# Loading twelve dense partial sums from another engine's queue, with a new table of ranks

## The chip, the core and the metric

The kernel runs on one core of one Trainium2 chip. The metric is the device time of one launch in microseconds (us). Three runs of the kernel before took 374.27, 373.19 and 374.27 us, so its time is 374.27 us (the median).

A core has five engines with instruction streams of their own: TensorE (PE, matrix products), VectorE (DVE), ScalarE (ACT), GpSimd (POOL) and SyncE (SP). Each takes its instructions strictly in the order in which they are written. Transfers (DMAs) are issued by an engine, here by SP and POOL, and then run beside it; a transfer that adds into its target is issued by POOL in this kernel.

## What is computed

The reference mixes, by a gate per row, a spectral filter and a two-layer perceptron. Shapes: A_x and B_x are 1 x 2048 x 512, w1 is 512 x 1792, w2 is 1792 x 512.

```python
x = A_x
g = _sigmoid((x * gate_w).sum(-1, keepdims=True))
X = jnp.fft.rfft2(x, axes=(-2, -1)) * (A_w_r + 1j * A_w_i)
a = jnp.fft.irfft2(X, s=(S, D), axes=(-2, -1))
h = jax.nn.gelu(jnp.einsum("bsd,df->bsf", B_x, w1) + b1, approximate=True)
b = jnp.einsum("bsf,fd->bsd", h, w2) + b2
return g * a + (1 - g) * b
```

Both reference branches see the same x here. Every product is made of three with split operands (a high and a low part: high x high, high x low, low x high).

## The kernel before

**How the work is cut.** The 2048 rows are four chunks of 512, `c` = 0 to 3. The 1792 hidden columns are 14 blocks of 128 (`f`), taken in two halves of seven. `mlp(half, c)` makes, for one chunk and one half, the up-projections `ph` (12 matmuls of 128 x 512 for each `f`), the gelu on ACT, the split into `g..h` (ACT) and `g..l` (DVE), and the down-projections `po` for four blocks `q` of 128 output columns (3 matmuls for each `f`). The first half's negated result goes to a buffer in device memory, `bacc[c]`. The second half's result is added to it there by POOL (`bacc<-o`), since no buffer on the chip holds it so long. The second halves run in the order of chunks 3, 0, 1, 2. The input of a chunk, split into `mxh` and `mxl`, exists once: the next chunk's, 1 MB each (`mxh<-xs2h`, `mxl<-xs2l` for chunk 2), may only be loaded once the last `ph` of the chunk before is done.

**The spectral part.** `forward` (16 blocks of rows) does the real transform along columns (`pd`) and rows (`py`) on PE; `stage1` and `filt` combine and filter on DVE; `stage4(c)` starts the inverse on DVE (names beginning with `d` and a digit, then `y`). `inverse(c, h)` makes for a half chunk two groups `pz` from `v..h` and `v..l` (PE; ACT makes `sw` and `v..h`, DVE `pq` and `v..l`), splits them into `z..h` and `z..l`, makes `pa` from those (PE), copies half of it to `od` (ACT), and takes sum and difference `uv` (DVE). The result goes to `out` by plain transfers on SP and by additions on POOL (`out<-uv`, `out<-y`).

**The step that is changed.** `combine(c, h)` (line 1037), called for chunks 3, 0 and 1, brings the finished dense sums back: for each of the two `k` it loads 256 KB of `bacc[c]` into a buffer `ba`, of which there are two slots. DVE scales it in place by the gate less one (line 1045). Then for chunks 3 and 0 POOL adds it to `out` (`out<-ba`), for chunk 1 with `h` = 0 SP writes it to `out` and the spectral part is added later, and for chunk 1 with `h` = 1 DVE adds it to `y` on the chip (line 1024). That is 3 x 2 x 2 = 12 loads. A load must wait for the two additions into `bacc` that it reads, and for its slot, which becomes free when the addition or write to `out` of the content before has landed.

**Chunk 2 is done last, and its end differs.** Its first-half result is loaded as `bb`. For `q` below 2 DVE makes `oo` from it (two buffers, lines 1142 and 1144) and POOL adds them to `out` (`out<-oo`). For `q` of 2 and 3 DVE makes the output tiles `o` (lines 1167 and 1172) from `po` and the finished `y`. `o` and `oo` share the two slots of one pool, `so`: the tile `o` of `q` = 2 may only be written once the transfer of the first `oo` has landed. The last matmuls of all are two groups of `po` for `q` = 3, each 256 wide (`po_230` and `po_23256`).

**What sets the order.** The program is first a list of 1,870 steps, each with its engine, its buffers and a rank. A planner (`Graph.schedule`) runs through estimated time and always starts, on each engine, the step of lowest rank among those whose inputs and slots are ready; the order that comes out is the order in which the instructions are written. The ranks come from a table, `RANKS`, one number for each step:

```python
for s, r in zip(g.steps, RANKS):
    s.rank = r / 100
order = g.schedule()
```

A step on SP takes part in the plan through `dma`, with at most 8 transfers in flight (`hw`); a step on POOL through `dma_pool` (plain) and `acc` (adding), with at most 3 in flight (`ring`).

Of the kernel before, what the change touches and what calls it, by code (L numbers as in the profile page):

```python
# [17 lines left out]
P = 128  # L18
# [154 lines left out]
class Graph:  # L173
# [282 lines left out]
def tile_kernel(ctx: ExitStack, tc: tile.TileContext, xt, w1, w2, b1, b2, x0g, wf, wrev, out, consts):  # L456
# [58 lines left out]
    def dma_pool(dst, src, kb, reads, writes, rank=FEED):  # L515
        reads = [*reads, buf("ring", [1], cls=len(g.steps))]
        return add("pool", kb / 300, 3.2, lambda: nc.gpsimd.dma_start(dst(), src()), reads, writes, rank)  # L517
# [772 lines left out]
```

## Time and profile before

The profile is of one more execution. A trace has a row for each instruction: its start, its duration, its line, what it writes and reads, and in brackets the time that its engine sat idle before it, with what ended that time.

| | |
|---|---|
| time, median of 3 runs (lowest, highest) | 374.27 us (373.19, 374.27) |
| the profiled execution's own time | 375.86 us |
| its span, first to last instruction | 374.1 us |
| mean granted TensorE clock | 0.998 |
| POOL busy, instructions | 53.2 us, 66 |
| loads `ba<-bacc` on POOL, each 256 KB | 12, first at 222.39 us, last at 347.94 us |
| DMA packets, bytes | 48564, 62.99 MB |

Three times stand beside one another: 375.86 us for the profiled execution, 374.1 us for its span, and 374.27 us for the median of the runs without a profile. A difference that is worked out from the trace is a difference in the first two.

### The profile page before, as it was taken

To read this page: it belongs to the slowest core of one execution; us is meant where nothing else is said; L and a number is where in the kernel's file an instruction comes from. 1 tells how busy PE (TensorE), PEld (TensorE's weight loads), DVE (VectorE), ACT (ScalarE), POOL (GpSimd) and SP (SyncE) were. 2 spreads that over 40 slices of the span, in tenths; PEclk is the share of its full clock that TensorE was granted. 3 is DMA by queue.
4 is the path that set the end of the run, shared out by engine and by line. 5 is a ranking of instruction groups with operands and counts; after the bars stand their busy time and mean duration, and the time that the engine had idled before them with its cause. 6 is when DMAs were issued, how large, how long until landed. Compare 5 with 4: busy or idle time off the path is not lost.

```text
span 374.1 us, 5563 instructions
## 1 busy us (share of the span) xinstructions
PE 365.5 (98%) x1838; PEld 310.0 (83%) x1838; DVE 326.6 (87%) x691; ACT 227.8 (61%) x454; POOL 53.2 (14%) x66
## 2 busy tenths in 40 slices
PE   7999999999999999999999999999999999999993
PEld 6888888888888888888888888888888877888893
DVE  4999999999999788999999999597758595999986
ACT  5766587876679735473467122984786449549820
POOL 0000000000000002011032021003323233312150
PEclk9999999999999999999999999999999999999999
DMA  8962799524965218479298952338958896854295
GB/s 284 377 183 89 213 289 337 169 84 141 268 191 152 64 16 218 120 162 229 66 232 206 308 79 43 57 109 239 208 96 145 191 286 163 129 102 123 86 128 153
DMA packets 48564, 62.99 MB, mean 168 GB/s; under 512 B 4656, under 2 KB 28272, under 8 KB 47760
## 3 DMA queue, kind: packets, MB, share of 16 engines
q1 hardware_dynamic: 40232, 46.39, 38.5%
q0 software_dynamic: 8160, 15.99, 26.0%
q8 instruction: 14, 0.23, 0.2%
q10 hardware_dynamic: 144, 0.26, 0.2%
q14 instruction: 14, 0.11, 0.1%
HBM read 38.64 MB, written 23.73 MB: 167 GB/s over the span
## 4 chain that ended last, share of the span: by engine, by line
PE 77%; DVE 8%; ACT 6%; DMA 6%; issue 2%; SPq 0%; DVEq 0%; POOL 0%; POOLq 0%; ACTq 0%
PE ph L530 35%; PE po L530 32%; PE pd L530 4%; PE py L530 3%; PE pz L530 2%; ACT sw L949 2%; PE pa L530 2%; DMA ba<-bacc 1%; DMA out<-oo 1%; DVE uv L1002 1%; DMA xr<-in_xt 1%; DMA out<-uv 1%; ACT sw L952 1%; DVE y L812 1%; DVE y L1021 1%
## 5 line engine op out<-in xcount | busy, mean ns | idle before, releaser
L1105 ACT ACTIVATE ph<-ph,b1t 128x512 f32<-128x512 f32 x56 | 36.7, 656 | 47.4 <-PE ph L530 47.3
L949 ACT ACTIVATE sw<-y,al 64x512 f32<-64x512 f32 x32 | 22.9, 722 | 3.3 <-DVE y L812 2.5
L521 POOL DMA_DIRECT2D wa7l<-in_w x1 | 1.0, 1007 | 141.3 <-PE po L530 141.3
L956 DVE SCALAR_TENSOR_TENSOR pq<-y,al,sw 128x256 f32<-128x256 f32 x32 | 14.6, 480 | 7.2 <-ACT sw L952 7.1
L908 DVE TENSOR_TENSOR m<-y,wf 128x514 f32<-128x514 f32 x32 | 20.6, 689 | 0.2
L521 POOL DMA_DIRECT2D bacc<-o x12 | 11.1, 926 | 54.2 <-ACT o L1154 54.2
L1154 ACT ACTIVATE o<-po 128x512 f32<-128x512 f32 x12 | 7.1, 594 | 15.4 <-PE po L530 15.4
L1151 ACT ACTIVATE o<-po,b2t 128x512 f32<-128x512 f32 x16 | 10.8, 684 | 9.0 <-PE po L530 8.9
L764 ACT ACTIVATE y<-pys 64x257 f32<-64x257 f32 x24 | 10.0, 418 | 5.4 <-DVE pys L761 5.0
L517 POOL DMA_DIRECT2D ba<-bacc x12 | 9.2, 764 | 26.3 <-DMA out<-ba 13.1
L530 PE MATMUL pd<-cf,eoh 128*128 128x260 f32 x64 | 12.6, 288 | 0.1
L1002 DVE TENSOR_TENSOR uv<-pa,od 128x512 f32<-128x512 f32 x16 | 10.4, 684 | 2.3 <-ACT od L999 2.3
L688 DVE TENSOR_TENSOR eo<-xr 128x256 f32<-128x256 f32 x30 | 12.0, 418 | 0.0
L530 PEld LDWEIGHTS pd<-cf,eoh 128*128 128x128 f32 x64 | 10.3, 189 | 1.2 <-issue 0.3
L999 ACT ACTIVATE od<-pa 128x512 f32<-128x512 f32 x8 | 4.8, 595 | 9.6 <-PE pa L530 9.4
L530 PE MATMUL pd<-cf,eol 128*128 128x130 f32 x64 | 10.4, 252 | 0.0
L952 ACT ACTIVATE sw<-y 1x512 f32<-1x512 f32 x16 | 10.0, 628 | 0.4
L530 PEld LDWEIGHTS pd<-cf,eol 128*128 128x128 f32 x64 | 9.8, 189 | 0.2
L702 DVE TENSOR_TENSOR xr<-eo 128x256 f32<-128x256 f32 x24 | 9.6, 418 | 0.1
L1045 DVE SCALAR_TENSOR_TENSOR ba<-gb,ba 128x512 f32<-128x512 f32 x12 | 8.2, 685 | 1.6 <-DMA ba<-bacc 1.6
L521 POOL DMA_DIRECT2D out<-ba x8 | 6.9, 863 | 15.9 <-DVE ba L1045 11.2
L650 DVE TENSOR_TENSOR mxl<-xm,mxh 128x512 fp32r<-128x512 f32 x12 | 7.8, 687 | 1.5 <-ACT mxh L649 1.5
(714 smaller groups left out, 1361.6 us busy)
## 6 DMA issues: line engine op xcount, KB each, us to landing
wf<-in_wf SPq DMA_DIRECT2D x16, 257.0 KB, 4.9
bacc<-o SPq DMA_DIRECT2D x16, 256.0 KB, 4.3
xr<-in_xt SPq DMA_DIRECT2D x15, 256.0 KB, 3.6
war<-in_w SPq DMA_DIRECT2D x14, 256.0 KB, 3.5
wbr<-in_w SPq DMA_DIRECT2D x14, 256.0 KB, 3.0
xm<-in_xt SPq DMA_DIRECT2D x12, 256.0 KB, 5.2
bacc<-o POOLq DMA_DIRECT2D x12, 256.0 KB, 4.1
ba<-bacc POOLq DMA_DIRECT2D x12, 256.0 KB, 3.4
```

The source lines that it names most:

```text
L521: return add("pool", kb / 150, 3.4, lambda: nc.gpsimd.dma_start(dst(), src(), accum_op=ALU.add), reads, writes, rank)
L530: pe.matmul(ps, w, x, start=start, stop=stop)
L688: v(lambda s=s, op=op: vec.tensor_tensor(eo.ap()[:, s], x.ap()[:, 0:2], x.ap()[:, 2:4], op=op), 256, [x], [(eo, s)], FEED)
L702: v(lambda k=k, op=op: vec.tensor_tensor(quarter(cl, k), eo.ap()[:, :, 0], eo.ap()[:, :, 1], op=op), 256, [eo], [(cl, k)] if j % 4 == 0 or ...
L764: a(lambda o=o, i=i: act.activation(Y[j].ap()[o:o + HP, 1], pys.ap()[i:i + HP, 1], AF.Copy), 257, [(pys, 1)], [(Y[j], 1 + k)], 0, more=0.1)
L908: v(lambda mk=mk, k=k, y=y, w=w: vec.tensor_tensor(mk.ap(), y.ap(), w.ap()[:, k:k + 1, :ND].to_broadcast([P, 2, ND]), op=ALU.mult), 514, [ ...
L949: a(lambda sw=sw, y=y, o=o, i=i: act.activation(sw.ap()[o:o + HP], y.ap()[i:i + HP, ::-1, :HD], AF.Copy, scale=al.ap()[i:i + HP, 0:1]), 51 ...
L952: a(lambda sw=sw, y=y, j=j: act.activation(sw.ap()[HP:HP + 1], y.ap()[HP:HP + 1, ::-1, :HD], AF.Copy, scale=math.cos(math.pi * j / NJ)), 5 ...
L956: v(lambda sw=sw, pq_=pq_, y=y, j=j, k=k, op=op: vec.scalar_tensor_tensor(pq_.ap()[:, k], y.ap()[:, k, :HD], al.ap()[:, 1 + j:2 + j], sw.a ...
L1002: v(lambda i=i, op=op: vec.tensor_tensor(uv.ap()[:, :, i], ps.ap()[:, 0], od.ap(), op=op), 512, [ps, od], [(uv, i)], 2)
L1105: a(lambda f=f, ps=ps: act.activation(ps.ap(), ps.ap(), AF.Gelu_apprx_tanh, bias=b1t.ap()[:, f:f + 1]), 600, [b1t], [ps], 0.9 if half else ...
L1151: a(lambda o=o, ps=ps, q=q: act.activation(o.ap(), ps.ap(), AF.Identity, scale=-1.0, bias=b2t.ap()[:, q:q + 1]), 600, [b2t, ps], [o])
```

## The change

`combine` issues its twelve loads of `bacc` by SP's queue and no longer by POOL's. The target, the source, the size and the declared dependences are the same. POOL is left with the adding transfers alone. All 1,870 numbers of `RANKS` are new, so the planner writes the whole program in another order; the steps themselves are the same.

```diff
 RANKS = (
-    71, 55, -369, -8, 46, 96, 146, 814, 1420, 458, 434, 906, 646, 2488, 2489, 832, 866, 912, 1011, 1123, 2161, 1407, 517,
...
+    -149, 43, 217, 3, 143, 100, 150, 574, 1118, 447, 437, 885, 624, 1856, 1001, 866, 832, 912, 1753, 1799, 1869, 396,
...
@@ combine(c, h)
         for k in range(2):
             b = buf("ba", [P, 2, 2 * P], F32, f"ba{k}{c}{h}")
-            dma_pool(lambda b=b: b.ap(), lambda k=k: bacc[c].ap()[2 * k:2 * k + 2, :, 2 * h * P:(2 * h + 2) * P].rearrange("q p n -> p q n"),
-                     256, [(bacc[c], 2 * q + h) for q in (2 * k, 2 * k + 1)], [b], 3)
+            dma(lambda b=b, k=k: sp.dma_start(
+                b.ap(), bacc[c].ap()[2 * k:2 * k + 2, :, 2 * h * P:(2 * h + 2) * P].rearrange("q p n -> p q n")),
+                256, [(bacc[c], 2 * q + h) for q in (2 * k, 2 * k + 1)], [b], 3)
```

What moves is seen in the written order at three places. In it `x2` marks a row that stands for two instructions, and the number behind a name is a buffer's.

**First place: PE, early, around the first down-projections.** The rows are the first of `po` and what follows them. Before:

```order
L530 MATMUL po_010_255<-g_0h,wb0h 128x512
L530 MATMUL po_010_255<-g_0l,wb0h 128x512
L530 MATMUL po_010_255<-g_0h,wb0l 128x512
L530 MATMUL ph_3_261<-mxh_110,wa3h 128x512
L530 MATMUL ph_3_261<-mxl_125,wa3h 128x512
```

And in the changed kernel:

```order
L530 MATMUL po_010_254<-g_0h,wb0h 128x512
L530 MATMUL po_010_254<-g_0l,wb0h 128x512
L530 MATMUL po_010_254<-g_0h,wb0l 128x512
L530 MATMUL po_010_254<-g_1h,wb1h 128x512
L530 MATMUL po_010_254<-g_1l,wb1h 128x512
L530 MATMUL po_010_254<-g_1h,wb1l 128x512
L530 MATMUL po_020_274<-g_0h,wb0h 128x512
```

The three rows that read `g_1` stood behind `ph_3` and `ph_4` and now stand right behind those of `g_0`.

**Second place: SP's queue and PE where chunk 2 takes over from chunk 1.** On SP before (`mxh` and `mxl` are chunk 2's input, `ti` small tables):

```order
L1015 DMA out<-uv_3332 128x512
L939 DMA ti_3359<-ti 128x128
L1015 DMA out<-uv_3332 128x512
L939 DMA ti_3418<-ti 128x128
L527 DMA mxh_3427<-xs2h 128x2048
L527 DMA mxl_3434<-xs2l 128x2048
```

And in the changed kernel:

```order
L1015 DMA out<-uv_3332 128x512
L1040 DMA ba_3360<-bacc_676 128x2x256
L1015 DMA out<-uv_3332 128x512
L1040 DMA ba_3388<-bacc_676 128x2x256
L939 DMA ti_3398<-ti 128x128
L527 DMA mxh_3430<-xs2h 128x2048
L527 DMA mxl_3441<-xs2l 128x2048
```

Two of the twelve loads now stand ahead of chunk 2's input in one queue. On PE a little later, before (`v2h` and `v2l` are the first operands that the inverse of chunk 2 makes):

```order
L530 MATMUL po_120_3523<-g_8h,wb8h 128x512
L530 MATMUL po_120_3523<-g_8l,wb8h 128x512
L530 MATMUL po_120_3523<-g_8h,wb8l 128x512
L530 MATMUL pz_3561<-tg_3280,v2h 128x256 x2
L530 MATMUL po_120_3523<-g_9h,wb9h 128x512
```

And in the changed kernel:

```order
L530 MATMUL po_120_3508<-g_12h,wb12h 128x512
L530 MATMUL po_120_3508<-g_12l,wb12h 128x512
L530 MATMUL po_120_3508<-g_12h,wb12l 128x512
L530 MATMUL pz_3589<-tg_3268,v2h 128x256 x2
L530 MATMUL pz_3589<-tg_3268,v2l 128x128 x2
```

Counted in the whole order, 42 matmuls of `po` stood between the last `ph` of chunk 1 and the first of chunk 2, and now 48; the first `pz` of `v2h` has moved back by 12 matmuls in all.

**Third place: POOL and DVE at the end.** POOL's last rows before:

```order
L521 DMA out<-uv_4024 128x512 x2
L521 DMA out<-oo_4054 128x512
L521 DMA out<-y 128x512
L521 DMA out<-oo_4085 128x512
L521 DMA out<-uv_4024 128x512
```

And in the changed kernel:

```order
L521 DMA out<-oo_4037 128x512
L521 DMA out<-uv_4045 128x512 x2
L521 DMA out<-oo_4063 128x512
L521 DMA out<-uv_4045 128x512
L521 DMA out<-y 128x512
```

DVE's last rows before:

```order
L1120 SCALAR_TENSOR_TENSOR bb_3947<-gb,bb_3947 128x512
L1167 SCALAR_TENSOR_TENSOR o_22_4116<-gb,po_220_4050 128x512
L1172 TENSOR_TENSOR o_22_4116<-y,o_22_4116 128x512
L1002 TENSOR_TENSOR uv_4135<-pa_4093,od_4122 128x2x256 x2
L1021 TENSOR_TENSOR y<-uv_4135 128x512 x2
L1123 TENSOR_TENSOR y<-y,bb_3947 128x2x256
L1024 TENSOR_TENSOR y<-y,ba_3971 128x512
L1024 TENSOR_TENSOR y<-y,ba_3881 128x512
L1167 SCALAR_TENSOR_TENSOR o_23_4175<-gb,po_230_4118 128x256
```

And in the changed kernel (one line was added, so line numbers are higher by one):

```order
L1121 SCALAR_TENSOR_TENSOR bb_3939<-gb,bb_3939 128x512
L1168 SCALAR_TENSOR_TENSOR o_22_4110<-gb,po_220_4033 128x512
L1173 TENSOR_TENSOR o_22_4110<-y,o_22_4110 128x512
L1124 TENSOR_TENSOR y<-y,bb_3939 128x2x256
L1002 TENSOR_TENSOR uv_4136<-pa_4100,od_4126 128x2x256 x2
L1021 TENSOR_TENSOR y<-uv_4136 128x512 x2
L1024 TENSOR_TENSOR y<-y,ba_3985 128x512
L1024 TENSOR_TENSOR y<-y,ba_3876 128x512
L1168 SCALAR_TENSOR_TENSOR o_23_4175<-gb,po_23256_4122 128x256
```

The first `out<-oo` now stands ahead of the two `out<-uv`, and the addition of `bb` to `y` ahead of the last `uv`. On PE, 39 matmuls of 256 columns follow the last `pa`, where 42 did.

216 rows, old and new, of the table RANKS are left out of this document.

## The prediction, made before the changed kernel was run

> **What bounds the kernel now.** The first view is the busy time of each engine, the second the same by stretches of the span (start and end, length, then busy time and instructions by engine, granted clock, DMA share, GB/s).
>
> ```profile
> PE 365.5 (98%) x1838; PEld 310.0 (83%) x1838; DVE 326.6 (87%) x691; ACT 227.8 (61%) x454; POOL 53.2 (14%) x66
> 9.20:130.00 120.80, 120.65 (x639) 103.77 (x640) 115.75 (x272) 87.38 (x216) 0.00 (x0) 1.00 0.65 198
> 130.00:285.00 155.00, 155.00 (x725) 129.82 (x724) 135.91 (x274) 87.32 (x149) 28.85 (x34) 1.00 0.61 148
> 285.00:320.00 35.00, 34.43 (x171) 28.46 (x170) 23.90 (x50) 22.04 (x38) 11.47 (x14) 1.00 0.88 203
> 320.00:363.50 43.50, 43.50 (x241) 37.83 (x240) 39.99 (x77) 25.70 (x45) 11.76 (x14) 1.00 0.58 112
> 363.50:374.10 10.60, 4.65 (x39) 4.44 (x38) 7.01 (x13) 0.24 (x1) 0.87 (x1) 0.93 0.63 151
> ```
>
> PE is the bound, and full: from 9.2 to 363.5 us it idles 0.15 + 0.57 = 0.7 us, at clock 1.00. The change neither adds nor removes a matmul. It can win only what PE still waits and what lies behind PE's last matmul, a couple of us; it can lose as much as it makes PE wait. POOL, whose queue is relieved, is busy 14%, so its busy time decides nothing. What matters is what the loads held up, and what they will hold up.
>
> The third view is the trace around the only idle stretch in PE's middle, on PE, SP and POOL, with the chain of waits through it (start, us, what).
>
> ```profile
> 305.94 0.39 PE L530 MATMUL ph<-mxh,wa7h 128*128 128x512 f32 x1
> 306.52 0.50 PE L530 MATMUL ph<-mxl,wa7h 128*128 128x512 f32 x1 [0.19 <-DMA mxl<-xs2l]
> 309.38 0.39 PE L530 MATMUL po<-g_8l,wb8h 128*128 128x512 f32 x1
> 309.61 0.39 PE L530 MATMUL po<-g_8h,wb8l 128*128 128x512 f32 x1
> 310.33 0.50 PE L530 MATMUL pz<-tg,v2h 128*128 128x256 f32 x2 [0.34 <-ACT v2h L576]
> ...
> 284.59 0.89 POOL L521 DMA_DIRECT2D out<-ba  x1 [0.22 <-issue]
> 292.40 0.88 POOL L521 DMA_DIRECT2D out<-y  x1 [4.65 <-ACT ph L1105]
> 293.14 0.89 POOL L517 DMA_DIRECT2D ba<-bacc  x1
> 295.53 0.42 SPq L527 DMA_DIRECT2D mxl<-xs2l  x1
> ...
> 287.05 4.68 DMA out<-uv
> 293.14 5.52 DMA ba<-bacc
> ...
> 298.76 0.69 DVE L1045 SCALAR_TENSOR_TENSOR ba<-gb,ba 128x512 f32<-128x512 f32 x1 [1.58 <-DMA ba<-bacc]
> ```
>
> A matmul of 512 columns starts 0.23 us after the one before it (309.38 to 309.61). Here two starts come late: 306.52 - 305.94 - 0.23 = 0.35 us, because chunk 2's input lands 11 us after its issue, and 310.33 - 309.61 - 0.23 = 0.49 us, because `v2h` is late. The chain says why `v2h` is: POOL's `out<-y` waited for a write of SP that landed at 291.73 (287.05 + 4.68), the load of `ba` stood behind it until 293.14 and took 5.52 us, and DVE, which scales `ba` before it starts the inverse of chunk 2, stood still for 1.58 us until it landed. So the queue that the change empties did cost PE time, in one place.
>
> The last view is the end: the chain, then DVE, ACT and PE in the trace.
>
> ```profile
> 357.96 5.48 DMA out<-oo
> ...
> 361.26 0.68 DVE L1120 SCALAR_TENSOR_TENSOR bb<-gb,bb 128x512 f32<-128x512 f32 x1
> 363.15 0.60 ACT L999 ACTIVATE od<-pa 128x512 f32<-128x512 f32 x1 [3.65 <-PE pa L530]
> 363.52 0.69 DVE L1167 SCALAR_TENSOR_TENSOR o<-gb,po 128x512 f32<-128x512 f32 x1 [1.58 <-DMA out<-oo]
> 364.25 0.69 DVE L1172 TENSOR_TENSOR o<-y,o 128x512 f32<-128x512 f32 x1
> 364.86 1.28 DVE L1002 TENSOR_TENSOR uv<-pa,od 128x512 f32<-128x512 f32 x2
> 367.38 0.69 DVE L1123 TENSOR_TENSOR y<-y,bb 128x512 f32<-128x512 f32 x1
> 367.99 1.29 DVE L1024 TENSOR_TENSOR y<-y,ba 128x512 f32<-128x512 f32 x2
> 369.19 0.74 DVE L1167 SCALAR_TENSOR_TENSOR o<-gb,po 128x256 f32<-128x256 f32 x2
> 369.85 0.76 DVE L1172 TENSOR_TENSOR o<-y,o 128x256 f32<-128x256 f32 x2
> 363.07 0.28 PE L530 MATMUL po<-g_7l,wb7h 128*128 128x256 f32 x1
> 363.19 0.28 PE L530 MATMUL po<-g_7h,wb7l 128*128 128x256 f32 x1
> 367.87 0.28 PE L530 MATMUL po<-g_13h,wb13l 128*128 128x256 f32 x1
> ```
>
> DVE stood 1.58 us until the first `out<-oo` had landed and freed the slot of `o`, and then ran without a break to 370.61. PE was done at 367.87 + 0.28 = 368.15. DVE is thus the last engine, about 1 us behind what PE alone would allow (369.19 against 368.15).
>
> **The change part by part.** *The twelve issues.* POOL loses 12 issues of 0.75 us, SP gains 12; the nearest row on SP, the load of `bb` (256 KB from the same buffer), issues in 0.33 us.
>
> ```profile
> L517 POOL DMA_DIRECT2D ba<-bacc x12 | 9.2, 764 | 26.3 <-DMA out<-ba 13.1 <-DMA bacc<-o 9.4 <-issue 3.9
> 346.17 0.33 SPq L1114 DMA_DIRECT2D bb<-bacc  x1
> ba<-bacc POOLq DMA_DIRECT2D x12, 256.0 KB, 3.4
> bb<-bacc SPq DMA_DIRECT2D x4, 256.0 KB, 3.0
> out<-ba POOLq DMA_DIRECT2D x8, 256.0 KB, 5.6
> ```
>
> They land in 3.4 us (median) from POOL, `bb` in 3.0 from SP. I take 0 for issue and landing: between 0.4 us less and nothing, twelve times, but DVE stands still for one of these loads only, in the row at 298.76 above; the others are covered by what DVE and PE do between (without that cover each would cost its 3 us). *The waits.* POOL stood 26.3 us in front of these loads. That wait does not vanish, it goes to SP, where the `uv` writes, the `ti` and the chunk inputs stand behind it; what this can cost is the second rival.
>
> The Trainium skill says, in "DMA: Bandwidth & Descriptors", section "SWDGE vs HWDGE vs iDMA", that starting transfers on several engines saves only the sequencer's time for starting them, which is usually small, since all run on the same DMA engines. By that rule the sum would be 0; by the rows the 4.65 us that POOL stood in front of `out<-y`, with a load behind it, is more than an issue.
>
> *Second place, PE's two late starts: -0.84 us.* In SP's queue the second load no longer stands behind `out<-y`. It needs the slot that the `out<-ba` of 284.59 frees; at the median of 5.6 us that is 290.2, against 293.14. DVE then need not stand 1.58 us, and the `pz` of `v2h` stands 12 x 0.23 = 2.7 us later on PE. Each alone exceeds 0.49. Chunk 2's input gets 6 more matmuls ahead of it, 1.36 us, against 0.35. Bounds: -0.53 us if only the idle time in brackets goes (0.19 + 0.34), -0.84 if the whole of both goes.
>
> *Third place, the end: -1.1 us.* On DVE the two rows of `uv` that stood ahead of the rows that make `oo` now stand behind, and so does a `v13l` that stood between: 3 rows of 0.61 us (367.38 to 367.99 is one). With `out<-oo` issued ahead of both `uv`, it starts 1.8 us sooner and lands at 357.96 + 5.48 - 1.8 = 361.6. Then DVE goes on after `bb` (361.26) at 0.61 us a row: `o` 361.87, `o` 362.48, `y` + `bb` 363.09, free at 363.70. `od` ends at 363.15 + 0.60 = 363.75, plus 3 x 0.12 us because 3 matmuls of 256 fewer follow `pa` (363.07 to 363.19 is one): 364.11. So `uv` starts at 364.15, not 364.86. From `uv` to the last `o` were 369.19 - 364.86 = 4.33 us; without the row of `bb` in it, 3.72: 367.87. The second of the last `o` must wait for PE's 368.15, so the two sums begin near 368.55, not 369.85. That is -1.3. If the `z` rows ahead of `bb` slip a little, only the 0.7 us at `uv` remain; I take -1.1, nearer the full amount, since each row but the transfer's own landing has its measured price. Next late would be PE itself.
>
> *First place and everything else: +0.4 us.* A new order of 1,870 steps makes waits that no row of before shows. Below: none, which is what 130 to 285 us had. Above: one load late by a landing, 3.2 us net (first rival). I take 0.4, near the 0.35 and 0.49 that this order's own two waits cost.
>
> Sum: -0.84 - 1.1 + 0.4 = -1.54 us. Against the profiled execution, 375.86 - 1.54 = 374.3 us (span 374.1 to 372.6). The median, 374.27, lies 1.6 us under that execution; taking the same difference, I forecast **372.7 us**.
>
> **The rivals.** *PE starves early (slower).* `g_1l` is now read right after the first `po`.
>
> ```profile
> 14.81 0.68 DVE L577 TENSOR_TENSOR g_1l<-ph,g_1h 128x512 fp32r<-128x512 f32 x1
> 15.62 0.39 PE L530 MATMUL po<-g_0h,wb0l 128*128 128x512 f32 x1
> 22.19 0.39 PE L530 MATMUL po<-g_1l,wb1h 128*128 128x512 f32 x1
> war<-in_w SPq DMA_DIRECT2D x10, 256.0 KB, 4.2
> ```
>
> DVE had it at 15.49 and PE read it at 22.19, 6.7 us to spare; PE will now read it at 15.62 + 2 x 0.23 = 16.08. DVE's own order brings it forward by one row of 256 (0.33 us): 0.9 us to spare. In the first 30 us a weight block takes 4.2 us to land; one needed there that comes a landing late leaves PE 4.2 - 0.9 = 3.3 us idle, and all behind it moves. From 1.54 + 0.9 = 2.4 us of lateness the change loses. 374.27 - 1.54 + 3.3 = 376.0 us. For it: DVE is 96% busy up to 130 us (115.75 of 120.80) and cannot catch up. Against: weights are loaded ahead of chunk 1's input in the new order.
>
> *SP is held by a load (slower).* `ba` stands ahead of chunk 2's input, which was issued at 295.15 to 295.53. The slot is free near 290.2, 5 us to spare, plus 1.36 us of `po`. If the addition before it lands one median (5.6 us) later than that, at 295.8, nothing shows; two later, at 301.4, PE waits 301.4 - 295.2 - 1.36 = 4.8 us: 374.27 - 1.1 + 4.8 = 378.0 us. It decides from about 7.5 us of lateness.
>
> *The wait only moves (no change).* If DVE and ACT do not turn the earlier `ba` into an earlier `v2h`, and the end's 1.58 us goes to `z` or `uv`, the -0.84 and most of the -1.1 fall away: 374.0 us. The runs without a profile, already 1.6 us shorter than the profiled one, may not have had these waits at all.
>
> By the skill's rule on several engines the outcome is this third rival's; the rows bear it out so far that eleven of the twelve loads held up no engine but POOL.
>
> **How the numbers follow.** A measurement tells about 0.3% from no change here, 1.1 us: faster is below 373.15, slower above 375.4. My forecast has 0.62, its own range 372.1 (all of -0.84 and -1.3, no new wait) to 374.0 (-0.53 - 0.7 + 1.0, the last a new wait as long as the two old ones and a little); of it 0.48 is faster, 0.14 the same. The rival without change has 0.16, of which 0.13 is the same. Early starving has 0.13, SP held 0.09, nearly all of both slower. Together: faster 0.48, same 0.27, slower 0.25. The range is 371.6 (half the spread of the three runs, 0.5 us, under the forecast's own) to 375.7 us; it leaves out the larger half of the two slower rivals.
>
> **What would show it.** In the changed profile PE's idle time between 285 and 320 us should be under 0.2 us (0.57 before); the load of `ba` should be in DVE's waits no more; the first `out<-oo` should be issued ahead of both `uv`, and DVE's `o` should not wait for it; PE's last matmul should end near 367.3 and DVE within 1 us of it. I am wrong if PE shows a new wait of more than 1 us, early on `po` or at chunk 2's first `ph`, or if SP stands before a `ba` load with a chunk's input behind it while PE idles.

## The result, and the profile after

| | before | after |
|---|---|---|
| median of 20 runs each (lowest to highest) | 374.27 us (373.19 to 375.17) | 372.73 us (371.84 to 373.72) |
| ratio, 95% interval | | 0.9958 [0.9948, 0.9968] |
| the profiled execution's own time, its span | 375.86 us, 374.1 us | 372.56 us, 370.8 us |

The changed kernel is faster by 0.42%, 1.54 us. The spans of the two profiled executions differ by 3.3 us, more than twice that: before's profiled execution lay above all of its 20 runs. Part of what its trace shows need not belong to its order, and the experiments had to find out which part.

The page's busy time of each engine after the change, and the loads' row among its DMA issues (count, size, median us to landing):

```profile
PE 365.1 (98%) x1838; PEld 309.9 (84%) x1838; DVE 327.5 (88%) x691; ACT 229.6 (62%) x454; POOL 44.1 (12%) x54
...
ba<-bacc SPq DMA_DIRECT2D x12, 256.0 KB, 3.2
```

The windows, with columns as in the prediction:

```profile
9.20:130.00 120.80, 120.80 (x640) 103.47 (x639) 115.73 (x272) 87.45 (x216) 0.00 (x0) 1.00 0.63 199
285.00:320.00 35.00, 35.00 (x178) 29.84 (x177) 27.53 (x57) 23.22 (x40) 9.25 (x11) 1.00 0.96 207
363.50:370.80 7.30, 2.90 (x25) 2.70 (x23) 4.01 (x9) 0.00 (x0) 0.45 (x1) 0.95 0.78 188
```

PE's idle 0.57 us between 285 and 320 us is gone, and so is the 0.15 us ahead of 130 us. The loads land in 3.2 us at the median, against 3.4. The second place in the trace of SP, POOL, DVE and PE:

```profile
287.55 0.37 SPq L1040 DMA_DIRECT2D ba<-bacc  x1
289.60 0.37 SPq L1040 DMA_DIRECT2D ba<-bacc  x1
295.26 0.47 SPq L527 DMA_DIRECT2D mxl<-xs2l  x1
...
290.82 0.88 POOL L521 DMA_DIRECT2D out<-y  x1 [5.34 <-ACT g_11h L576]
...
293.21 0.69 DVE L1046 SCALAR_TENSOR_TENSOR ba<-gb,ba 128x512 f32<-128x512 f32 x1 [0.31 <-DMA ba<-bacc]
...
307.27 0.39 PE L530 MATMUL ph<-mxl,wa7h 128*128 128x512 f32 x1
```

And the view of the tile `xs2l`, the second half of chunk 2's input, with its landing (lowest, median and highest of one transfer):

```profile
DMA to landing us min/median/max: 10.8/10.8/10.8
```

The second load goes out at 289.60 us, ahead of POOL's `out<-y`, and DVE waits 0.31 us for it instead of 1.58. Chunk 2's input lands at 295.26 + 10.8 = 306.1 us, 1.2 us ahead of its use. The end on POOL, DVE and PE:

```profile
354.47 0.86 POOL L521 DMA_DIRECT2D out<-oo  x1 [13.53 <-DVE oo L1145]
356.27 1.78 POOL L521 DMA_DIRECT2D out<-uv  x2 [0.94 <-DVE uv L1002]
...
360.31 0.68 DVE L1168 SCALAR_TENSOR_TENSOR o<-gb,po 128x512 f32<-128x512 f32 x1
362.40 1.29 DVE L1002 TENSOR_TENSOR uv<-pa,od 128x512 f32<-128x512 f32 x2
366.80 0.75 DVE L1173 TENSOR_TENSOR o<-y,o 128x256 f32<-128x256 f32 x2
...
366.13 0.28 PE L530 MATMUL po<-g_13h,wb13l 128*128 128x256 f32 x1
```

`o` waits for nothing now. PE's last matmul ends at 366.13 + 0.28 = 366.41 us (368.15 before) and DVE at 367.55, 1.14 us behind it (2.46 before).

### The profile page after: what moved, and what is told of

It reads as the page before. It is cut to its first block, busy times and chain, and to the rows that moved or that the text cites. A ratio compares the mean times of both kernels' runs of the same rounds, so it can differ in the third digit from the quotient of the medians.

```text
span 370.8 us, 5565 instructions
## 1 busy us (share of the span) xinstructions
PE 365.1 (98%) x1838; PEld 309.9 (84%) x1838; DVE 327.5 (88%) x691; ACT 229.6 (62%) x454; POOL 44.1 (12%) x54
## 4 chain that ended last, share of the span: by engine, by line
PE 95%; DVE 1%; DMA 1%; issue 0%; ACT 0%; SPq 0%; DVEq 0%
PE ph L530 41%; PE po L530 40%; PE pz L530 4%; PE pd L530 4%; PE py L530 3%; PE pa L530 3%; DMA xr<-in_xt 1%; DVE uv L1002 0%; DVE y L1021 0%; SPq L588 0%; DVE y L1024 0%; DVE mxl L650 0%; DVE o L1168 0%; ACT mxh L649 0%; ACT od L999 0%
## 5 line engine op out<-in xcount | busy, mean ns | idle before, releaser
L530 PE MATMUL pd<-cf,eoh 128*128 128x260 f32 x64 | 12.7, 285 | 0.0
L649 ACT ACTIVATE mxh<-xm 128x512 fp32r<-128x512 f32 x12 | 6.9, 623 | 3.7 <-PE ph L530 3.7
L705 DVE TENSOR_TENSOR eol<-xr,eoh 128x512 fp32r<-128x512 f32 x12 | 8.3, 688 | 0.2
```

The source lines that it names most:

```text
L530: pe.matmul(ps, w, x, start=start, stop=stop)
```

## The experiments

All compute the same values; only queues and orders differ. Medians are of the run's own 5 to 12 executions, ratios are to the kernel before on the same chip. The runs were made on three chips: the first four rows on one; queue_only, second_only, end_undone and cover_undone on another; one_load, load_back, cover_36 and cover_54 on a third. Two runs from different chips are better compared by their ratios than by their medians.

| run | loads on | order | median, us | ratio [95%] |
|---|---|---|---|---|
| before_again | POOL | before | 374.65 | 1.0000 [0.9986, 1.0014] |
| after_again | SP | after | 372.80 | 0.9948 [0.9930, 0.9966] |
| loads_only | SP | planned from the old ranks | 378.60 | 1.0091 [1.0067, 1.0114] |
| ranks_only | POOL | planned from the new ranks | 373.06 | 0.9954 [0.9940, 0.9969] |
| queue_only | SP | before, step for step | 373.57 | 0.9956 [0.9938, 0.9974] |
| one_load | POOL | before, one load moved | 373.94 | 0.9982 [0.9970, 0.9994] |
| load_back | POOL | ranks_only, that load moved back | 374.91 | 0.9998 [0.9982, 1.0014] |
| second_only | POOL | before, five steps of PE moved | 374.88 | 1.0006 [0.9989, 1.0023] |
| end_undone | SP | after, two steps of the end moved back | 375.86 | 1.0025 [1.0011, 1.0038] |
| cover_undone | SP | after, 42 products ahead of chunk 2 | 373.66 | 0.9963 [0.9950, 0.9976] |
| cover_36 | SP | after, 36 products | 376.08 | 1.0033 [1.0014, 1.0052] |
| cover_54 | SP | after, 54 products | 372.87 | 0.9947 [0.9935, 0.9959] |

### Both kernels once more

No edit.

> The kernel before, profiled and timed a second time. Theory (its waits belong to its order): median 374.3 us, ratio 1.000; in the profile PE's late starts at chunk 2's first product and at the product of v2h come again (PE idle between 285 and 320 us 0.4 to 0.7 us) and DVE ends 2 to 2.5 us behind PE's last matmul. Rival (the profiled execution was a bad draw, 1.6 us over the median, and had waits that most executions do not have): span of the new profile near 372.5 us, PE idle there below 0.2 us, DVE's end 1 to 1.5 us behind PE's.

> The changed kernel, profiled and timed a second time beside the others on the same chip. Theory: ratio 0.996 (372.7 us), span of the profile 370.8 to 371.3 us, no late start of PE over 0.15 us between 285 and 320 us. Rival (the first measurement's 1.5 us was the chip): ratio 0.999 or above.

The late start on PE, and the middle and the end on DVE, in the second profile's trace of before:

```profile
308.49 0.39 PE L530 MATMUL po<-g_8h,wb8l 128*128 128x512 f32 x1
309.48 0.50 PE L530 MATMUL pz<-tg,v2h 128*128 128x256 f32 x2 [0.60 <-ACT v2h L576]
...
297.91 0.69 DVE L1045 SCALAR_TENSOR_TENSOR ba<-gb,ba 128x512 f32<-128x512 f32 x1 [1.35 <-DMA ba<-bacc]
361.38 0.69 DVE L1167 SCALAR_TENSOR_TENSOR o<-gb,po 128x512 f32<-128x512 f32 x1 [0.29 <-PE po L530]
368.00 0.75 DVE L1172 TENSOR_TENSOR o<-y,o 128x256 f32<-128x256 f32 x2
...
367.02 0.28 PE L530 MATMUL po<-g_13h,wb13l 128*128 128x256 f32 x1
```

PE's last matmul ends at 367.02 + 0.28 = 367.30 us. The wait for `ba` (1.35 us) and the late `pz` (309.48 - 308.49 - 0.23 = 0.76 us) come again; they belong to the order. The late start at chunk 2's input does not, and DVE stands only 0.29 us at `o`: its end lies 368.00 + 0.75 - 367.30 = 1.45 us behind PE. Each expectation was half right here: the middle recurs, most of the end's 1.58 us does not. After_again repeats the changed kernel.

### The loads alone, the ranks alone

loads_only has the change's new call of `dma` in `combine` with the old `RANKS`; ranks_only has the new `RANKS` with the old call of `dma_pool`.

> The twelve loads on SyncE's queue, with the order (ranks) of before. Theory (second place comes from the queue, third place from the order): PE's two late starts near 306 and 310 us go or shrink below 0.2 us together, DVE no longer waits 1.58 us for a load of ba, the end stays (DVE about 2.5 us behind PE's last matmul): 0.5 to 0.85 us below before, ratio 0.998. Rival (the ranks carry all of it, the queue nothing): ratio 1.000, the 0.49 us at v2h's product stays.

> The loads on GpSimd's queue as before, with the order (ranks) of after. Theory: the end is won (DVE 1 to 1.5 us behind PE's last matmul), and at the second place v2h's product stands 12 matmuls later, so that its late start goes as well although the load of ba stays late: 1.1 to 1.5 us below before, ratio 0.996 to 0.997, that is nearly all of the change's gain. Rival (the queue is needed): the load of ba in this order waits longer on GpSimd, PE starts late again by 0.5 us or more near 310 us, and the ratio is 0.998 or above.

The ranks alone give 0.9954, within the interval of the whole change. With them the queue is worth nothing that can be measured. The loads alone, planned anew, are slower by 0.9%, which neither theory had. PE's trace in loads_only, at chunk 2's input and at the inverse of chunk 1:

```profile
305.38 0.39 PE L530 MATMUL ph<-mxh,wa7h 128*128 128x512 f32 x1
307.72 0.63 PE L530 MATMUL ph<-mxl,wa7h 128*128 128x512 f32 x1 [1.95 <-DMA mxl<-xs2l]
308.15 0.63 PE L530 MATMUL ph<-mxh,wa7l 128*128 128x512 f32 x1
...
352.31 0.34 PE L530 MATMUL pz<-tg,v5l 128*128 128x128 f32 x2
354.65 0.74 PE L530 MATMUL pa<-z10h,ci 128*128 128x256 f32 x4 [2.00 <-ACT z10h L976]
356.09 0.80 PE L530 MATMUL pa<-z10l,ci 128*128 128x256 f32 x2 [0.70 <-DVE z10l L979]
```

One microsecond's window behind the first stall:

```profile
309.00:310.00 1.00, 1.00 (x4) 0.81 (x3) 0.00 (x0) 0.99 (x2) 0.00 (x0) 0.50 0.54 156
```

There are two stalls. At the input PE starts 307.72 - 305.38 - 0.23 = 2.11 us late (1.95 us of it idle). At `pa` it is idle for 2.00 us and soon for 0.70 us more; there the planner left nothing between the last `pz` and the product that needs its result. With each, the granted clock falls to 0.50 for a while: products follow at 308.15 - 307.72 = 0.43 us, not 0.23.

### The queue alone, in the old order

The planner counts the loads on POOL as before; SP issues them.

```diff
-            dma_pool(lambda b=b: b.ap(), lambda k=k: bacc[c].ap()[2 * k:2 * k + 2, :, 2 * h * P:(2 * h + 2) * P].rearrange("q p n -> p q n"),
-                     256, [(bacc[c], 2 * q + h) for q in (2 * k, 2 * k + 1)], [b], 3)
+            add("pool", 256 / 300, 3.2, lambda b=b, k=k: sp.dma_start(
+                b.ap(), bacc[c].ap()[2 * k:2 * k + 2, :, 2 * h * P:(2 * h + 2) * P].rearrange("q p n -> p q n")),
+                [*[(bacc[c], 2 * q + h) for q in (2 * k, 2 * k + 1)], buf("ring", [1], cls=len(g.steps))], [b], 3)
```

> The order of before on every engine, step for step, with the twelve loads issued by SyncE at the places where GpSimd issued them. Theory (the queue moves a wait from v2h's product to chunk 2's input): DVE's wait for a load of ba near 298 us (1.35 to 1.58 us in before) falls below 0.5 us and v2h's product starts on time, but the second half of chunk 2's input now lands 11 to 13 us after its issue (10.8 to 12.7 in the three runs with the loads on SyncE), with 42 products ahead of it PE waits 0.3 to 2.1 us there, and with more than about 2 us of it the following ten products run at half the clock: 374.5 to 377.5 us, ratio 1.000 to 1.008. Rival (the queue itself is harmless, the loss of the loads alone came from the order that the planner made of the old ranks): ratio 0.997 to 0.999, no wait of PE at the chunk's input.

SP's second load and DVE's use of it in the trace of queue_only:

```profile
290.14 0.37 SPq L1040 DMA_DIRECT2D ba<-bacc  x1
...
296.71 0.68 DVE L1046 SCALAR_TENSOR_TENSOR ba<-gb,ba 128x512 f32<-128x512 f32 x1
```

Its window of the second place:

```profile
285.00:320.00 35.00, 35.00 (x176) 29.72 (x176) 25.56 (x53) 22.91 (x40) 8.02 (x10) 1.00 0.94 209
```

And the landing of `xs2l`:

```profile
DMA to landing us min/median/max: 8.6/8.6/8.6
```

The rival was nearer: with the old order kept, the queue alone is 1.3 us faster, DVE waits no more for the load, PE shows no late start, and the input lands in time. This run and loads_only both have the loads on SP and differ in order alone, so the 5 us between them (ratios 0.9956 and 1.0091) come from the order that the planner made, not from the queue. How the order does it is seen for the stall at `pa` only. At chunk 2's input both runs have 42 `po` products ahead, and what differs in the two profiles is the landing: 8.6 us here, 12.7 us in loads_only, for a reason that stays open. The profiled execution of queue_only (372.39 us) is also the fastest of its eight, the slowest of which took 374.64 us, so others may have landed later. Queue and ranks each bring the gain of the middle, and together they bring it once.

### One load, moved and moved back

Here and below, `put` takes a step out of the written order and sets it ahead of or behind another. Step 1595 is the second load of `ba` for chunk 0, half 0; step 1257 is the `out<-y` that waited in front of it. one_load (before) and load_back (ranks_only):

```diff
     order = g.schedule()
+    put(1595, ahead=1257)
```

```diff
     order = g.schedule()
+    put(1595, behind=1257)
```

> The kernel before with one row of GpSimd's queue moved: the second load of ba for chunk 0, half 0, ahead of the addition of y that waits for a write's landing, not behind it. Theory (the whole gain of the middle is this one load, which the new queue and the new ranks each bring ahead of that wait): DVE's wait for it (1.35 to 1.58 us) falls below 0.7 us, no late start of PE above 0.2 us between 285 and 320 us, 0.8 to 1.4 us below before, ratio 0.996 to 0.998, that is what the queue alone gave (0.9956). Rival (the load was a part only): PE still late by 0.4 us or more there, ratio 0.999 or above.

> The loads on GpSimd with the new ranks (0.9954 of before), and the same load put back behind the addition of y. Theory: DVE waits 1 us or more for the load near 296 us again, and although v2h's product stands later, a late start of PE of 0.4 to 0.9 us comes back between 285 and 320 us, perhaps at a po product that waits for ACT; ratio to before 0.997 to 0.998. Rival (the new places on PE cover it): no late start of PE, ratio 0.995 to 0.996.

POOL and DVE in the trace of one_load:

```profile
290.71 0.75 POOL L517 DMA_DIRECT2D ba<-bacc  x1 [2.63 <-DMA out<-uv]
291.46 0.95 POOL L521 DMA_DIRECT2D out<-y  x1
...
297.07 0.68 DVE L1045 SCALAR_TENSOR_TENSOR ba<-gb,ba 128x512 f32<-128x512 f32 x1
```

The same two rows of POOL in ranks_only, where the new ranks have the load ahead:

```profile
289.98 0.75 POOL L517 DMA_DIRECT2D ba<-bacc  x1 [1.66 <-DMA out<-ba]
291.10 0.92 POOL L521 DMA_DIRECT2D out<-y  x1 [0.37 <-issue]
```

And in the trace of load_back, the load, DVE's wait and two of PE's late starts:

```profile
292.37 0.88 POOL L517 DMA_DIRECT2D ba<-bacc  x1
...
298.56 0.69 DVE L1045 SCALAR_TENSOR_TENSOR ba<-gb,ba 128x512 f32<-128x512 f32 x1 [6.22 <-DMA ba<-bacc]
...
299.90 0.50 PE L530 MATMUL po<-g_12l,wb12h 128*128 128x512 f32 x1 [0.52 <-DVE g_12l L577]
313.74 0.51 PE L530 MATMUL pz<-tg,v6h 128*128 128x256 f32 x2 [0.52 <-ACT v6h L576]
```

One row of POOL's queue takes DVE's wait away (no time in brackets at 297.07), and 0.76 us off the median (373.94 against 374.70 of before beside it), a little less than expected; PE's longest late start between 285 and 320 us is 0.16 us. The same row put back costs the new ranks all that they had won: 0.9998, more than expected. That is not the wait of before restored: in the new order DVE reaches the load earlier, so it stands 6.22 us for it, where before it stood 1.58, and load_back overstates what the row cost before. The two runs show from both sides that the row's place decides the middle; its price in the old order is what one_load measured, 0.76 us (0.2 to 1.1 by the interval). Whether one_load's 0.76 us really are less than queue_only's 1.3 is open: the intervals overlap.

### PE's places alone

Five groups of three `po` products of chunk 1 set ahead: two ahead of chunk 2's first product (1781), three ahead of the `pz` of `v2h` (1325). PE then has the changed kernel's places there: 48 products ahead of chunk 2's first, and the first `pz` of `v2h` 12 matmuls later than before.

```diff
     order = g.schedule()
+    put(1653, ahead=1781)
+    put(1654, ahead=1781)
+    put(1655, ahead=1325)
+    put(1656, ahead=1325)
+    put(1657, ahead=1325)
```

> The kernel before, loads on GpSimd, with five steps of PE moved: two groups of three po products ahead of chunk 2's first product, and three ahead of v2h's. Theory (PE's late starts at the second place are its products' places, not the queue): both late starts go, 0.5 to 1.0 us below before, ratio 0.9975 to 0.9985, the end as in before. Rival (the loads must leave GpSimd's queue): v2h's product still starts late by 0.3 us or more, ratio 0.999 to 1.000.

DVE at the load and PE at its late start in the trace of second_only:

```profile
298.48 0.69 DVE L1045 SCALAR_TENSOR_TENSOR ba<-gb,ba 128x512 f32<-128x512 f32 x1 [1.48 <-DMA ba<-bacc]
...
316.39 0.50 PE L530 MATMUL po<-g_7h,wb7h 128*128 128x512 f32 x1 [0.68 <-ACT o L1154]
```

Nothing is won, and neither expectation had it so. DVE still stands 1.48 us for the load, and PE's late start has moved from the `pz` to a `po` whose accumulator ACT had not yet emptied. Later places on PE only move the wait; the earlier load removes it.

### The end

The first `out<-oo` (1831) back behind both `uv` writes, and `y` + `bb` (1849) back behind `y` = `uv`, in the changed kernel.

```diff
     order = g.schedule()
+    put(1831, behind=1733)
+    put(1849, behind=1773)
```

> The changed kernel with the end put back in two steps: the first addition of oo issued behind both additions of uv, and the addition of bb to y behind both rows y = uv. Theory of the prediction (the end is worth 1.1 us): DVE stands at o until the first addition of oo has landed, its end lies 2 us or more behind PE's last product, 0.7 to 1.3 us above the changed kernel, ratio to before 0.998 to 0.999. Rival (before's 1.58 us at o belonged to its first profiled execution, the second had 0.29): at most 0.3 us above the changed kernel, ratio 0.995 to 0.996.

POOL and DVE in the trace of end_undone:

```profile
356.48 1.77 POOL L521 DMA_DIRECT2D out<-uv  x2 [15.33 <-DVE uv L1002]
357.69 1.46 POOL L521 DMA_DIRECT2D out<-oo  x1
...
364.33 0.69 DVE L1168 SCALAR_TENSOR_TENSOR o<-gb,po 128x512 f32<-128x512 f32 x1 [3.73 <-DMA out<-oo]
```

This costs about 2.9 us against the changed kernel (ratios 1.0025 and 0.9948), above both theories: since DVE's rows of `uv` stay behind `oo` here, the write waits for `uv` until 357.69 us, 3.2 us later than in the changed kernel. It shows that the place of `out<-oo` bounds the end, but not what before's end cost. That is read from the profiles: DVE ended 1.45 to 2.46 us behind PE in the six with before's end (2.46, 1.45, 1.75, 1.48, 1.51, 2.04, mean 1.78) and 1.14 or 1.15 in all seven others with the new one. By these profiles the new end is worth 0.63 us on average, and is steadier; no run moves the end of before alone.

### The cover of chunk 2's input

In the changed kernel, chunk 2's first product (1781) six or twelve products earlier, or six later:

```diff
     order = g.schedule()
+    put(1781, ahead=1655)
```

```diff
     order = g.schedule()
+    put(1781, ahead=1647)
```

```diff
     order = g.schedule()
+    put(1649, ahead=1781)
+    put(1656, ahead=1781)
```

> The changed kernel, loads on SyncE, with chunk 2's first product six po products earlier (42 ahead of it, as in before, not 48). Theory (with the loads on SyncE the new order is needed, since the chunk's input lands later): PE waits at the second half of the input, which landed 0.4 to 1.2 us ahead of its use, by 0.2 to 1.0 us; ratio to before 0.996 to 0.998, 0.2 to 1.0 us above the changed kernel. Rival (the input would land as early as it is wanted; the cover is spare): no wait above 0.15 us there, ratio 0.995.

> The changed kernel with chunk 2's first product twelve po products earlier (36 ahead of it, not 48): 1.36 us less cover than the run with 42, whose profile had 1.51 us of wait there. Theory (a stall of over about 2 us is paid twice, as in the run with the loads alone: 2.11 us of wait and then ten products at 0.43 us, not 0.23): a wait of 1.5 to 2.9 us, and behind it, where it is over 2 us, products at 0.43 us for 4 us or so, 2 to 5 us above the changed kernel, ratio 1.000 to 1.008. Rival (a stall costs its own length): products at 0.23 us right behind it, 1.5 to 2.5 us above, ratio 0.999 to 1.002.

> The changed kernel with 54 po products ahead of chunk 2's first, not 48: 1.36 us more between the issue of its input and its use. Theory (in some executions the input lands later than its 0.4 to 1.2 us of spare): the slower executions go, the median 0.1 to 0.5 us below the changed kernel, ratio to before 0.993 to 0.9945. Rival (the cover is enough, and the later ph2 product makes the steps behind it late): 0 to 0.5 us above it, ratio 0.995 to 0.996.

PE's trace with 42 products ahead (cover_undone):

```profile
306.21 0.39 PE L530 MATMUL ph<-mxh,wa7h 128*128 128x512 f32 x1
307.95 0.50 PE L530 MATMUL ph<-mxl,wa7h 128*128 128x512 f32 x1 [1.34 <-DMA mxl<-xs2l]
308.28 0.40 PE L530 MATMUL ph<-mxh,wa7l 128*128 128x512 f32 x1
308.52 0.40 PE L530 MATMUL ph<-mxh,wa7h 128*128 128x512 f32 x1
```

And with 36 (cover_36):

```profile
304.56 0.39 PE L530 MATMUL ph<-mxh,wa7h 128*128 128x512 f32 x1
307.35 0.80 PE L530 MATMUL ph<-mxl,wa7h 128*128 128x512 f32 x1 [2.41 <-DMA mxl<-xs2l]
307.94 0.63 PE L530 MATMUL ph<-mxh,wa7l 128*128 128x512 f32 x1
308.37 0.63 PE L530 MATMUL ph<-mxh,wa7h 128*128 128x512 f32 x1
```

Two windows of cover_36 behind the stall:

```profile
309.00:310.00 1.00, 1.00 (x3) 0.79 (x3) 0.15 (x1) 0.98 (x2) 0.04 (x1) 0.50 0.73 185
311.00:312.00 1.00, 1.00 (x6) 0.78 (x5) 0.39 (x1) 0.97 (x2) 0.38 (x1) 1.00 1.21 209
```

With 42 products the stall is 307.95 - 306.21 - 0.23 = 1.51 us in the profile, and the products behind it follow at 0.24 us. But the profiled execution (374.57 us) lies 0.9 us above its run's median; by the ratios, 0.9963 and 0.9948, the run is 0.6 us above the changed kernel, and the intervals overlap. With 36 products the stall is 307.35 - 304.56 - 0.23 = 2.56 us, and the products behind it start 0.43 us apart until the clock is back, about 1.6 us more. Here the ratios are clear: 1.0033 against 0.9948, 3.2 us. The profile's 2.56 + 1.6 = 4.2 us is more, but its execution (377.19 us) lies 1.1 us above the median; the twelve runs spread from 374.32 to 377.72 us, and how many of them lost the clock, one profile does not tell. So at least part of the cover is needed, and the profile bears out the theory that a longer stall costs more than its length. More cover (cover_54) brings nothing: ratio 0.9947 against 0.9948. In its profile the input took 12.7 us to land, 0.7 us ahead of its use, so with 1.36 us less of cover PE would, as an estimate, have stood 0.7 us; and its five runs lie close together (372.53 to 373.06). Five are too few to call that a gain.

## Why the prediction was right

The forecast of 372.7 us came true to 0.1 us, and its two main terms come about in the way that it named. That it came so near is luck: two of its terms were wrong by 0.5 and 0.7 us, in opposite directions. Step by step:

- **Issues and landing, 0.** Right: 3.2 against 3.4 us to landing, and in the changed kernel's two profiles DVE waits for one of the twelve alone, 0.31 and 0.51 us.
- **The second place, -0.84.** Right in size: the two late starts (0.84 us) and a third of 0.2 us at 317.99 us are gone, and in the second pair of profiles 0.76 + 0.18 = 0.94 us; in the medians the one row was worth 0.76 us (one_load). Right too that the load stood behind `out<-y`. Wrong was the sentence "Each alone exceeds 0.49", which took the later `pz` for a second, independent remedy: second_only shows that it only moves the wait. And what brings the load forward need not be the queue. The new ranks also put it ahead of `out<-y` when POOL issues it, which ranks_only and load_back show, and which the prediction did not see because it compared only SP's new place with POOL's old one.
- **The end, -1.1.** The mechanism held: the first `out<-oo` went out 366.41 - 354.47 = 11.94 us ahead of PE's end, against 368.15 - 357.96 = 10.19 us before, so 1.75 us sooner where 1.8 were forecast. The size did not hold: about -0.63 us (0.3 to 1.3). The step that failed took DVE's 1.58 us at `o`, seen in one execution, as the order's standing price. The second profile had 0.29.
- **First place and everything else, +0.4.** The wrong sign. No new wait came, and a late start near 41 us that every profile with the old ranks has (two rows of `pd` 0.46 to 0.49 us apart in six, where the same two rows a group later are 0.17 to 0.18 us apart) is in none of the eight with the new ones: about -0.3 us. This is read from the traces alone; no run moves it by itself.
- **The sum.** With the terms as read from the profiles it is -0.94 - 0.63 - 0.3 = -1.9 us; the two comparisons of medians gave -1.54 and -2.0 us. Carrying the difference from the profiled execution over to the median came out right only because the end's term was 0.5 us too large and the last one 0.7 us off the other way: the two profiled executions themselves differ by 3.3 us.
- **The signs.** Of those named, PE's idle time in the middle (none), the place of `out<-oo` and the free `o` came as said. Missed were DVE's wait for the load, which shrank but did not vanish, and the end: PE finished at 366.41 us, not near 367.3, with DVE 1.14 us behind it, not within 1.

The rivals. *PE starves early* did not happen: `g_1l` is written from 14.37 us for 0.68 us and read at 15.85, 0.8 us to spare where 0.9 were forecast. *SP is held* did not happen either; 5.3 us lay between the load's issue (289.60) and that of the chunk's input. The danger lay next to it, in the landing of that input, which left 0.4 to 1.2 us in the two profiles of the changed kernel, and the 1.36 us of cover, booked against 0.35 us, carry more than was thought. *The wait only moves* is what second_only did. The Trainium skill's rule ("DMA: Bandwidth & Descriptors", "SWDGE vs HWDGE vs iDMA") that issuing from several engines saves little but issue time agrees with ranks_only against after_again, 373.06 and 372.80 us; in the old order the queue alone was worth 1.3 us (queue_only), and there the rule does not count what stands in front of a transfer in its queue. The rule is about the queue and not about the new order, so the prediction's "By that rule the sum would be 0" asked more of it than it says.

## What to carry to other kernels

When a transfer is late, look at what stands ahead of it in its queue and what that waits for: moving one row there gave 0.76 us here, about half of what the new queue (1.3 us) or the new ranks (1.75 us) gave alone. Price a wait from two or more profiled executions, above all when the profiled one is slower than its runs. After a change of queue, plan anew with care: the same queue gave -1.3 us in the old order and +3.8 us in the order that the planner made of the old ranks.

## What the runs showed of the hardware

A stall of PE of about 2 us cost more than its length. In three places PE stood idle for 1.95 us, for 2.00 and 0.70 us in close succession (both loads_only), and for 2.41 us (cover_36). Each time the granted clock fell to 0.50 for 3.4 us, worked out from windows of 1 us (in cover_36, 0.66, 0.50, 0.50 and 0.64 between 307 and 311 us), and products of 512 columns took 0.43 us, not 0.23: 1.6 us more behind the first and the last of them. The fall came 2.2, 3.1 and 2.4 us after PE had stopped. After 1.34 us of idle time (cover_undone) the clock stayed at 1.00. Where between 1.34 and 1.95 us the limit lies, and whether the moment of the stall counts beside its length, four stalls do not tell. The Trainium skill ("TensorE: Matmul & The Clock Gate", "Part 1: The HAM clock gate") has the same half rate, but after at least one idle window of about 3.4 us; here less idle time than that sufficed.

The 1 MB second half of chunk 2's input took between 8.6 and 12.7 us from issue to landing in the runs that show it, with the same queue and nearly the same time of issue (294.9 to 295.8 us). What makes the difference was not settled.
